# A unit's difference ahead of the low half of the unit in front, with other banks, pages and load times at the changes of stages and blocks

## The chip, the cores and the metric

The kernel runs on one core of a Trainium2 chip. The metric is the device time of one execution in microseconds (us), as the median of several runs. The core's engines work in parallel, each through its own queue in order: TensorE (PE; PEld is its loading of weights), VectorE (DVE), ScalarE (ACT), GpSimd (POOL) and SyncE (SP). SP and ACT also issue the DMA transfers.

## The reference

A linear attention with a normalisation of each row feeds two feed-forward layers, one behind the other, on 4608 tokens of width 512 with 2048 hidden channels:

```python
kv = einsum('bhsd,bhse->bhde', k, v); out = einsum('bhsd,bhde->bhse', q, kv)
x = out / sqrt(mean(out * out) + 1e-06) * g_norm      # then tokens x (heads * dim)
h = x @ w_in;  x = (h * sigmoid(h)) @ w_out           # moe
h = x @ w_in2; r = maximum(h, 0)
y = (s * (r * r) + b) @ w_out2                        # moe2
```

All is float32.

## The kernel before

**Numbers.** TensorE multiplies in a rounded format (`F32R`). To keep float32 accuracy each operand is split into a high half, the rounded value, made by ACT (`nc.scalar.copy`), and a low half, the value minus its high half, made by DVE (`nc.vector.tensor_sub`). A product is then three passes (`PASSES`, line 556): high by high, high by low, low by high.

**Stages.** There are four: stage 1 is the attention and `x @ w_in` with its activation (`emit_h`, in nine steps `j` of 512 tokens, 16 column groups `m` each); stage 2 is `@ w_out` (class `Output`); stage 3 is the second `@ w_in` with its activation (class `Hidden`); stage 4 the second `@ w_out` (`Output` again). Stages 2 to 4 work on five blocks of tokens, in the order 1, 2, 3, 4, 0: four long ones of two times 512 and a short one of two times 256. Each 2 by 2 block product there is done as seven products instead of eight (Strassen's scheme in Winograd's form), named in the order of their use P1, P5, P6, P2, P7, P4, P3. They add up in three kinds of PSUM banks, x, v and y: P1 and P2 in x, P5 and P3 in v, P6, P7 and P4 in y, to which x is copied first.

**The loop of stages 2 and 4** (`Output.run`, line 845). Its unit is a product k and one of NA = 4 groups a of channels, 28 units a block, 12 matmuls a unit (two halves q of the output, two channel groups i, three passes). `load` issues a unit's loads on SP, seven units ahead: r for P5, P2 and P7 into four pages in turn (`R_ROOMS`), sa for P6, ka for P1. `make` (line 763) makes the operand of a unit three units ahead into one of four slots (`RING`, one for each a): for P5, P6 and P7 first a difference on DVE (lines 774, 776, 778), then the high half on ACT (line 780) and the low half on DVE (line 781). For P2 the kept operand `ka` is changed behind the low half (line 783). At the end of a product `end_of` (line 819) copies or adds the banks: line 833 copies y at the end of P7, line 834 adds v, line 794 scales in stage 4, line 840 adds v and u at the end of P3. In stage 4 `rows_out` transposes finished rows (line 810), copies them on ACT (line 812) and stores them.

**Stage 3** (`Hidden.run`, line 690) goes through 40 groups g = (block, i), seven slots each, 6 matmuls a slot. P4 and P3 of a group come one group later. The operands of a block (7 splits into halves) are made by `split` (line 591), their sums T1, T2, T4 and B12 by `combine` (line 578). For the first block `before` (line 607) does that during the last, short block of stage 2; for the others `behind` does it in the last group of the block in front. Results go into a page (`G_ROOMS`, line 562, four in turn) by `square` on ACT or `add_square` on ACT and DVE (lines 685 to 688), and `defer` puts the store's issue on ACT's queue some slots later (`run_late`, once a slot). Between the slots the weights of stage 4 are prepared in small steps (`steps4`, called in `beside3`, line 936), and weight tiles are loaded (`grid[..].load`, line 312).

**Order.** All is in a manual schedule: each engine does its instructions in the order in which the code emits them; the framework adds the waits. A page or bank with a tag has one owner at a time, so a new owner waits until the last reader of the old one is done.

Of the kernel before, what the change touches and what calls it, by code (L numbers as in the profile page):

```python
# [8 lines left out]
F32 = mybir.dt.float32  # L9
# [8 lines left out]
def kernel(  # L18
# [37 lines left out]
    P = 128  # L56
# [402 lines left out]
    def emit_h(j, m):  # L459
# [8 lines left out]
        g = room(("gh_0", "gh_1", "gl_0", "gl_1")[m % 4], [P, T], F32, f"g{j}_{m}")  # L468
# [89 lines left out]
    class Hidden:  # L558
# [3 lines left out]
        G_ROOMS = ("sg_0", "sg_1", "sg_2", "v_1")  # L562
# [15 lines left out]
        def combine(self, b, o):  # L578
# [5 lines left out]
            elif o == self.T2:  # L584
                to, x, y = self.raw[b, self.T1], B22, self.raw[b, self.T1]
            else:
                to, x, y = self.raw[b, self.T2], self.raw[b, self.B21], self.raw[b, self.T2]
# [19 lines left out]
        def before(self, k, a):  # L607

            b = order[0]
            if (k, a) == (P7, 3):  # L610
                for o in (self.B11, self.B12, self.B22, self.B21):
                    self.load(b, o)
            if (k, a) == (P4, 1):
                self.combine(b, self.T1)
            if (k, a) == (P3, 0):
                self.split(b, P1)
            if (k, a) == (P3, 1):
                self.split(b, P5)
                self.combine(b, self.T2)
                self.split(b, P6)  # L620
            if (k, a) == (P3, 2):
                self.split(b, P2)
                self.combine(b, self.B12)
            if (k, a) == (P3, 3):
                self.split(b, P7)
# [44 lines left out]
        def out(self, g, f, h):  # L670
            b = self.seq[g][0]
            self.turn += 1
            r = room(self.G_ROOMS[self.turn % 4], [P, T], F32, f"g{b}_{f}_{h}")[:, :size[b]]
            defer(2 if b else 4, lambda: nc.scalar.dma_start(self.gt[b][f, h], r))
            return r

        def square(self, g, f, h, ps):
            r = self.out(g, f, h)
# [3 lines left out]
        def add_square(self, g, f, h, x, y):  # L682
            r = self.out(g, f, h)
# [37 lines left out]
    class Output:  # L721


        def __init__(self, stage):
            self.stage, self.grid, self.gt = stage, grid[stage], gt[stage - 1]
            self.units = [(b, k, a) for b in order for k in range(7) for a in range(NA)]
            self.loaded = self.made = 0
            self.s, self.r, self.o, self.acc, self.c, self.waiting = {}, {}, {}, {}, {}, []
            self.turn = 0
            self.keep, self.t = {}, []  # L730
            self.c_rooms = ["gh_0", "kvw1_0", "sg_2" if stage == 2 else "T", "v_0", "v_1", "sg_0", "sg_1", "gl_1"]
# [31 lines left out]
        def make(self, upto):  # L763
            while self.made < min(upto, len(self.units)):
                u = self.made
                self.made += 1
                b, k, a = self.units[u]
                n = size[b]
                o = self.o[u] = room(RING[a], [P, 2, 2, T], F32R, f"o{self.stage}_{u}")[:, :, :, :n]
                keep = self.kept(a, n)  # L770
                r = self.r.pop(u, None)
# [7 lines left out]
                x = r if k in (P2, P7) else s if k == P3 else keep  # L779
# [301 lines left out]
```

## Time and profile before

| | us |
|---|---|
| median of 3 runs | 1670.33 (1666.95 to 1672.37) |
| profiled execution | 1665.62 |
| its span | 1663.5 |
| PE matmul busy | 1593.3 |
| DVE busy | 957.2 |
| ACT busy | 802.5 |

The profile is of one execution. In a timeline a row is a run of like instructions: start, time, engine, line, operation, output and inputs, count, and in brackets the idle time of the engine just before it and what ended it. Matmuls overlap by some 0.15 us, so a row's time is longer than the distance to the next row's start. In a grouped row stand the busy time, the mean of one instruction, and the idle time before them with what ended it. The granted clock is a share of 2.4 GHz.

### The profile page before, as it was taken

How to read it: one execution, taken by the hardware profiler on the slowest of the kernel's cores; microseconds unless marked ns; L12 is line 12 of the kernel's file. 1: busy time of each engine (PE TensorE's matmuls, PEld its weight loads, DVE VectorE, ACT ScalarE, POOL GpSimd, SP SyncE). 2: the span in 40 equal slices, each digit the busy share in tenths (PEclk: the TensorE clock that was granted, in tenths of full speed). 3: DMA queues.
4: the chain of work that ended last, by engine and by line, in shares of the span. 5: the costliest groups of instructions: out<-in, count | busy, mean ns of one | idle time of the engine just before them, and what ended most of it. 6: DMA issues, size and time to landing. Idle time of an engine off the chain costs nothing.

```text
span 1663.5 us, 22083 instructions
## 1 busy us (share of the span) xinstructions
PE 1593.3 (96%) x8232; PEld 1309.2 (79%) x8232; DVE 957.2 (58%) x1298; ACT 802.5 (48%) x1310; POOL 1.6 (0%) x8
## 2 busy tenths in 40 slices
PE   7999999999899999999998999999989999999998
PEld 5778877888788778778787778787888787878787
DVE  5625544554321767676756666667545757575745
ACT  3645544555333343444444565656554454545454
POOL 0000000000000000000000000000000000000000
PEclk9999999999999999999999999999999999999999
DMA  8977887788829552626259747565467662626241
GB/s 240 279 221 255 277 269 253 244 287 264 329 83 335 182 215 89 228 78 240 80 197 360 279 179 260 189 238 195 184 236 288 251 237 67 225 66 236 65 152 51
DMA packets 228074, 349.60 MB, mean 210 GB/s; under 512 B 59008, under 2 KB 96896, under 8 KB 227968
## 3 DMA queue, kind: packets, MB, share of 16 engines
q1 hardware_dynamic: 145504, 209.49, 38.6%
q10 hardware_dynamic: 82464, 138.71, 22.3%
q8 instruction: 65, 1.06, 0.3%
q14 instruction: 41, 0.34, 0.1%
HBM read 209.72 MB, written 138.41 MB: 209 GB/s over the span
## 4 chain that ended last, share of the span: by engine, by line
PE 51%; DVE 21%; ACT 11%; DMA 10%; issue 5%; ACTq 1%; SPq 1%; DVEq 0%
PE ph L465 18%; DVE o L781 9%; PE qy L858 8%; ACT o L780 8%; PE py L662 7%; PE qv L858 5%; PE pv L662 4%; DMA gt<-g 4%; PE px L662 4%; DVE r L778 3%; DVE ka L774 3%; DVE ka L776 2%; DVE ka L783 1%; PE pkv L346 1%; PE po L371 1%
## 5 line engine op out<-in xcount | busy, mean ns | idle before, releaser
L858 PE MATMUL qy<-o,w 128*128 128x512 f32 (+1 forms) x1440 | 314.4, 373 | 23.8 <-DVE o L781 18.2
L858 PEld LDWEIGHTS qy<-o,w 128*128 128x128 f32 x1440 | 248.9, 188 | 86.3 <-DVE o L781 35.5
L781 DVE TENSOR_TENSOR o<-ka,o 128x1024 fp32r<-128x1024 f32 (+1 forms) x160 | 177.0, 1117 | 199.0 <-ACT o L780 188.3
L780 ACT CAST o<-ka 128x1024 fp32r<-128x1024 f32 (+1 forms) x160 | 152.0, 963 | 203.3 <-DVE ka L776 91.7
L858 PE MATMUL qv<-o,w 128*128 128x512 f32 (+1 forms) x960 | 203.5, 369 | 1.5 <-ACT o L780 0.9
L858 PE MATMUL qx<-o,w 128*128 128x512 f32 (+1 forms) x960 | 203.8, 370 | 0.0
L858 PEld LDWEIGHTS qv<-o,w 128*128 128x128 f32 x960 | 167.1, 189 | 31.5 <-ACT o L780 1.1
L858 PEld LDWEIGHTS qx<-o,w 128*128 128x128 f32 x960 | 168.0, 190 | 29.9
L662 PE MATMUL py<-x,w 128*128 128x512 f32 (+1 forms) x720 | 164.9, 374 | 12.2 <-ACT g L685 9.2
L465 PE MATMUL ph<-xh,wh 128*128 128x512 f32 x576 | 166.1, 410 | 6.9 <-ACT xh L443 5.3
L469 ACT ACTIVATE g<-ph 128x512 f32<-128x512 f32 x144 | 86.1, 598 | 150.6 <-PE ph L465 145.9
L662 PEld LDWEIGHTS py<-x,w 128*128 128x128 f32 x720 | 127.0, 191 | 39.6 <-ACT g L685 11.5
L465 PE MATMUL ph<-xl,wh 128*128 128x512 f32 x576 | 155.7, 392 | 0.0
L465 PE MATMUL ph<-xh,wl 128*128 128x512 f32 x576 | 154.5, 390 | 0.0
L780 ACT CAST o<-r 128x1024 fp32r<-128x1024 f32 (+1 forms) x80 | 75.0, 962 | 110.9 <-DVE r L778 110.9
L465 PEld LDWEIGHTS ph<-xl,wh 128*128 128x128 f32 x576 | 108.6, 189 | 24.6 <-DVE xl L444 0.4
L465 PEld LDWEIGHTS ph<-xh,wl 128*128 128x128 f32 x576 | 108.3, 188 | 23.4
L465 PEld LDWEIGHTS ph<-xh,wh 128*128 128x128 f32 x576 | 101.0, 189 | 27.2 <-ACT xh L443 6.8
L662 PE MATMUL pv<-x,w 128*128 128x512 f32 (+1 forms) x480 | 113.8, 373 | 5.1 <-issue 4.4
L781 DVE TENSOR_TENSOR o<-r,o 128x1024 fp32r<-128x1024 f32 (+1 forms) x80 | 89.3, 1116 | 44.0 <-ACT o L780 44.0
L662 PE MATMUL px<-x,w 128*128 128x512 f32 (+1 forms) x480 | 111.9, 369 | 0.0
L662 PEld LDWEIGHTS pv<-x,w 128*128 128x128 f32 x480 | 85.8, 192 | 21.3 <-issue 4.8
(114 smaller groups left out, 1635.5 us busy)
## 6 DMA issues: line engine op xcount, KB each, us to landing
gt<-g ACTq DMA_DIRECT2D x272, 256.0 KB, 2.6
r<-gt SPq DMA_DIRECT2D x96, 512.0 KB, 4.4
w<-wd SPq DMA_DIRECT2D x84, 512.0 KB, 6.6
wd<-wo ACTq DMA_DIRECT2D x112, 256.0 KB, 4.2
wr<-in_moe_w_in_dram SPq DMA_DIRECT2D x16, 1024.0 KB, 6.1
wr<-in_moe_w_out_dram SPq DMA_DIRECT2D x16, 1024.0 KB, 5.4
ka<-gt SPq DMA_DIRECT2D x32, 512.0 KB, 5.3
sa<-gt SPq DMA_DIRECT2D x32, 512.0 KB, 8.5
```

The costliest lines, as they stand in the source:

```text
L346: nc.tensor.matmul(ps[r, r], kc, vc, start=(c == 0), stop=(c == SC))
L371: nc.tensor.matmul(po[off:off + n, p * P:(p + 1) * P], qT_t[t][:, p, off:off + n], kvw[b % 2][:, p, :], start=True, stop=True,)
L465: nc.tensor.matmul(ps, wt[:, c, :], xt[:, c, :], start=(n == 0 and c == 0), stop=(n == 2 and c == KT - 1))
L469: nc.scalar.activation(g, ps, AF.Silu)
L662: nc.tensor.matmul(ps, a[:, s, c], x[t][c], start=(k in (P1, P5) and n == c == 0), stop=(n == 2 and c == 1), skip_group_check=True,)
L774: nc.vector.tensor_sub(keep, r, keep)
L776: nc.vector.tensor_sub(keep, s, keep)
L778: nc.vector.tensor_sub(r, s, r)
L780: nc.scalar.copy(o[:, :, 0], x)
L781: nc.vector.tensor_sub(o[:, :, 1], x, o[:, :, 0])
L783: nc.vector.tensor_sub(keep, r, keep)
L858: nc.tensor.matmul(ps, t[:, s], self.o[u][:, i, p], start=(k in (P1, P5) and a == i == m == 0), stop=(a == NA - 1 and i == 1 and m == 2), ...
```

## The change

- `Output.make` is cut in two. `prepare` makes a unit's difference, for P2 also the changed `ka`; `make` makes the halves. In `run` the next unit's `prepare` is called between a unit's high and low half, so on DVE a unit's difference stands ahead of the low half of the unit in front.
- In stage 2 the v banks are y2 and y3 instead of y0 and y1.
- The operands of stage 3's first block are loaded two units sooner; T2 gets a page of its own for that block, and T1, T2, the P6 split and B12 move to the P4 units; one split is left for each P3 unit.
- Stage 3's results in the short block go through seven pages instead of four, their stores are issued 3 or 4 slots later instead of 4; in the long blocks the stores of `add_square` 3 slots later instead of 2. One weight step less is done in each long block, at the last but one group's P4.
- Stage 1's results go through eight pages instead of four, and in the last step but one through twelve of their own.

```diff
         def run(self, behind):
             for u, (b, k, a) in enumerate(self.units):
                 self.load(u + 7)
-                self.make(u + 4)
+                self.make(u + 4, 1)
...
-        def make(self, upto):
+        def prepare(self, upto):
+            while self.prepared < min(upto, len(self.units)):
+                u = self.prepared
+                self.prepared += 1
+                self.load(u + 1)
...
                 elif k == P7:
                     nc.vector.tensor_sub(r, s, r)
-                x = r if k in (P2, P7) else s if k == P3 else keep
+                elif k == P2:
+                    nc.vector.tensor_sub(keep, r, keep)
+                self.x[u] = r if k in (P2, P7) else s if k == P3 else keep
+
+        def make(self, upto, ahead=0):
+            while self.made < min(upto, len(self.units)):
+                u = self.made
+                self.made += 1
+                self.prepare(u + 1)
...
                 nc.scalar.copy(o[:, :, 0], x)
+                self.prepare(u + 1 + ahead)
                 nc.vector.tensor_sub(o[:, :, 1], x, o[:, :, 0])
-                if k == P2:
-                    nc.vector.tensor_sub(keep, r, keep)
...
-                        self.acc[kind, q] = bank(f"a_{q}" if kind == "x" else f"y{q}_0", f"q{kind}{self.stage}_{b}_{q}")
+                        self.acc[kind, q] = bank(f"a_{q}" if kind == "x" else f"y{self.v0 + q}_0", f"q{kind}{self.stage}_{b}_{q}")
...
+            self.v0 = 2 if stage == 2 else 0
...
-            if (k, a) == (P7, 3):
+            if (k, a) == (P7, 1):
                 for o in (self.B11, self.B12, self.B22, self.B21):
                     self.load(b, o)
-            if (k, a) == (P4, 1):
-                self.combine(b, self.T1)
-            if (k, a) == (P3, 0):
-                self.split(b, P1)
-            if (k, a) == (P3, 1):
-                self.split(b, P5)
-                self.combine(b, self.T2)
+            if k == P4 and a < 2:
+                self.combine(b, (self.T1, self.T2)[a])
+            if (k, a) == (P4, 2):
                 self.split(b, P6)
-            if (k, a) == (P3, 2):
-                self.split(b, P2)
                 self.combine(b, self.B12)
-            if (k, a) == (P3, 3):
-                self.split(b, P7)
+            if k == P3:
+                self.split(b, (P1, P5, P2, P7)[a])
...
-                to, x, y = self.raw[b, self.T1], B22, self.raw[b, self.T1]
+                to = pair("wf_0", f"xt2_{b}")[:, :, :size[b]] if b == order[0] else self.raw[b, self.T1]
+                x, y = B22, self.raw[b, self.T1]
...
-        G_ROOMS = ("sg_0", "sg_1", "sg_2", "v_1")
+        G_ROOMS = ("sg_0", "sg_1", "sg_2", "v_1", "v_0", "kvw1_0", "gh_0")
...
-            r = room(self.G_ROOMS[self.turn % 4], [P, T], F32, f"g{b}_{f}_{h}")[:, :size[b]]
-            defer(2 if b else 4, lambda: nc.scalar.dma_start(self.gt[b][f, h], r))
+            r = room(self.G_ROOMS[self.turn % (4 if b else 7)], [P, T], F32, f"g{b}_{f}_{h}")[:, :size[b]]
+            defer(slots if b else slots + 1, lambda: nc.scalar.dma_start(self.gt[b][f, h], r))
             return r
 
         def square(self, g, f, h, ps):
-            r = self.out(g, f, h)
+            r = self.out(g, f, h, 2)
...
         def add_square(self, g, f, h, x, y):
-            r = self.out(g, f, h)
+            r = self.out(g, f, h, 3)
...
-            if 0 < i < NF - 1 and k not in (P1, P3):
+            if 0 < i < NF - 1 and k not in (P1, P3) and (i, k) != (NF - 2, P4):
                 do_some(steps4, 1)
...
-        g = room(("gh_0", "gh_1", "gl_0", "gl_1")[m % 4], [P, T], F32, f"g{j}_{m}")
+        pages = ("gh_0", "gh_1", "gl_0", "gl_1")
+        if j < NB - 2:
+            pages += ("W4", "W5", "W6", "W7")
+        tag = f"W{m}" if j == NB - 2 and m < 3 * NA else pages[m % len(pages)]
+        g = room(tag, [P, T], F32, f"g{j}_{m}")
```

## Rows read from the trace of the kernel before

**Rows 1.** The page: busy us, share of the span and instructions of each engine.

```profile
PE 1593.3 (96%) x8232; PEld 1309.2 (79%) x8232; DVE 957.2 (58%) x1298; ACT 802.5 (48%) x1310; POOL 1.6 (0%) x8
```

**Rows 2.** Timeline of PE in stage 2, as described above.

```profile
536.72 11.04 PE L858 MATMUL qx<-o,w 128*128 128x512 f32 x48
547.60 11.04 PE L858 MATMUL qv<-o,w 128*128 128x512 f32 x48
...
569.27 2.79 PE L858 MATMUL qy<-o,w 128*128 128x512 f32 x11 [0.54 <-DVE o L781]
...
647.92 2.79 PE L858 MATMUL qy<-o,w 128*128 128x512 f32 x11 [0.55 <-DVE o L781]
...
872.32 5.92 PE L858 MATMUL qx<-o,w 128*128 128x256 f32 x48
878.08 3.47 PE L858 MATMUL qy<-o,w 128*128 128x256 f32 x25
```

**Rows 3.** Timeline of PE from stage 2 to stage 3.

```profile
897.07 1.55 PE L662 MATMUL px<-x,w 128*128 128x512 f32 x6
903.00 2.90 PE L662 MATMUL pv<-x,w 128*128 128x512 f32 x6 [4.38 <-issue]
```

**Rows 4.** Grouped lines of PE in stage 2 (536 to 897.2 us).

```profile
L858 PE MATMUL qy<-o,w 128*128 128x512 f32 (+1 forms) x720 | 156.2, 372 | 8.6 <-DVE o L781 8.5
```

**Rows 5.** Timeline of DVE in stage 2: units of P6, then of P2.

```profile
557.33 1.23 DVE L781 TENSOR_TENSOR o<-ka,o 128x1024 fp32r<-128x1024 f32 x1 [1.19 <-ACT o L780]
558.47 1.22 DVE L776 TENSOR_TENSOR ka<-sa,ka 128x1024 f32<-128x1024 f32 x1
560.88 1.23 DVE L781 TENSOR_TENSOR o<-ka,o 128x1024 fp32r<-128x1024 f32 x1 [1.19 <-ACT o L780]
...
570.27 1.22 DVE L783 TENSOR_TENSOR ka<-r,ka 128x1024 f32<-128x1024 f32 x1
571.40 1.22 DVE L781 TENSOR_TENSOR o<-r,o 128x1024 fp32r<-128x1024 f32 x1
```

**Rows 6.** Grouped lines of PE in stage 4 (from 1268 us).

```profile
L858 PE MATMUL qy<-o,w 128*128 128x512 f32 (+1 forms) x720 | 158.2, 373 | 15.1 <-DVE o L781 9.7 <-ACT c L833 5.4
```

**Rows 7.** Timeline of ACT at the end of P7 in a block of stage 4.

```profile
1413.17 0.81 ACT L794 ACTIVATE c<-c,sums,scol 128x512 f32<-128x512 f32 x1 [1.94 <-DVE c L834]
```

**Rows 8.** The page's DMA issues: count, KB each, median us to landing.

```profile
r<-gt SPq DMA_DIRECT2D x96, 512.0 KB, 4.4
```

**Rows 9.** Windows: busy us of PE, PEld, DVE, ACT, POOL, then clock, DMA share, GB/s.

```profile
903.00:908.30 5.30, 5.30 (x13) 4.14 (x14) 2.60 (x3) 1.29 (x2) 0.00 (x0) 0.50 1.04 410
```

**Rows 10.** Timeline of DVE at the end of stage 2.

```profile
890.53 1.23 DVE L589 TENSOR_TENSOR xt<-xs,xs 128x1024 f32<-128x1024 f32 x1 [1.87 <-DMA xs<-yt]
...
902.48 0.75 DVE L840 TENSOR_TENSOR c<-qv,qu 128x256 f32<-128x256 f32 x2
```

**Rows 11.** Timeline of SP's DMA issues at the end of stage 2.

```profile
881.87 4.61 SPq L576 DMA_DIRECT2D xs<-yt  x4
```

**Rows 12.** Timeline of PE at a change of blocks in stage 3.

```profile
1139.70 3.09 PE L662 MATMUL py<-x,w 128*128 128x512 f32 x12 [1.07 <-ACT g L685]
```

**Rows 13.** Timeline of ACT just before that.

```profile
1138.11 1.05 ACT L604 CAST x<-xs 128x1024 fp32r<-128x1024 f32 x1 [2.11 <-DVE g L688]
```

**Rows 14.** Grouped lines of PE in stage 3's short block (1213 to 1262 us).

```profile
L662 PE MATMUL py<-x,w 128*128 128x256 f32 (+1 forms) x149 | 22.5, 295 | 5.2 <-ACT g L685 2.6 <-ACT u L706 2.6
```

**Rows 15.** Waits of ACT there (1215 to 1270 us): total, times, longest.

```profile
ACT g L679 <- DMA gt<-g: 11.5, 6, 4.0
```

**Rows 16.** Timeline of PE at the end of stage 3.

```profile
1265.60 1.65 PE L662 MATMUL py<-x,w 128*128 128x256 f32 x6 [3.39 <-ACT g L685]
```

**Rows 17.** Timeline of ACT just before that.

```profile
1263.47 1.04 ACT L780 CAST o<-ka 128x1024 fp32r<-128x1024 f32 x1 [1.40 <-DMA ka<-gt]
1265.18 0.37 ACT L685 COPY g<-py 128x256 f32<-128x256 f32 x1 [0.66 <-DMA gt<-g]
```

**Rows 18.** Grouped lines of PE over the whole span: stage 1's first pass.

```profile
L465 PE MATMUL ph<-xh,wh 128*128 128x512 f32 x576 | 166.1, 410 | 6.9 <-ACT xh L443 5.3 <-ACT g L469 1.6
```

More of the change, by code (lines that the diff above doesn't have):

```diff
@@ L668, in of, with out @@
             return self.banks[kind, g][:, :size[self.seq[g][0]]]
-        def out(self, g, f, h):
+        def out(self, g, f, h, slots):
             b = self.seq[g][0]
             self.turn += 1
-            r = room(self.G_ROOMS[self.turn % 4], [P, T], F32, f"g{b}_{f}_{h}")[:, :size[b]]
-            defer(2 if b else 4, lambda: nc.scalar.dma_start(self.gt[b][f, h], r))
+            r = room(self.G_ROOMS[self.turn % (4 if b else 7)], [P, T], F32, f"g{b}_{f}_{h}")[:, :size[b]]
+            defer(slots if b else slots + 1, lambda: nc.scalar.dma_start(self.gt[b][f, h], r))
             return r
         def square(self, g, f, h, ps):
-            r = self.out(g, f, h)
+            r = self.out(g, f, h, 2)
             nc.scalar.activation(r, ps, AF.Relu)
@@ L726, in __init__ @@
             self.units = [(b, k, a) for b in order for k in range(7) for a in range(NA)]
-            self.loaded = self.made = 0
-            self.s, self.r, self.o, self.acc, self.c, self.waiting = {}, {}, {}, {}, {}, []
+            self.loaded = self.prepared = self.made = 0
+            self.s, self.r, self.x, self.o, self.acc, self.c, self.waiting = {}, {}, {}, {}, {}, {}, []
             self.turn = 0
             self.keep, self.t = {}, []
+            self.v0 = 2 if stage == 2 else 0
             self.c_rooms = ["gh_0", "kvw1_0", "sg_2" if stage == 2 else "T", "v_0", "v_1", "sg_0", "sg_1", "gl_1"]
@@ L761, in load @@
                     )
-        def make(self, upto):
-            while self.made < min(upto, len(self.units)):
-                u = self.made
-                self.made += 1
+        def prepare(self, upto):
[3 more added lines that the diff above has]
+                self.load(u + 1)
                 b, k, a = self.units[u]
                 n = size[b]
-                o = self.o[u] = room(RING[a], [P, 2, 2, T], F32R, f"o{self.stage}_{u}")[:, :, :, :n]
-                keep = self.kept(a, n)
-                r = self.r.pop(u, None)
+                keep, r = self.kept(a, n), self.r.get(u)
                 s = self.s[a][:, :, :n] if a in self.s else None
@@ L778, in make @@
                     nc.vector.tensor_sub(r, s, r)
-                x = r if k in (P2, P7) else s if k == P3 else keep
+                elif k == P2:
[6 more added lines that the diff above has]
+                self.prepare(u + 1)
+                b, k, a = self.units[u]
+                o = self.o[u] = room(RING[a], [P, 2, 2, T], F32R, f"o{self.stage}_{u}")[:, :, :, :size[b]]
+                x = self.x.pop(u)
                 nc.scalar.copy(o[:, :, 0], x)
+                self.prepare(u + 1 + ahead)
                 nc.vector.tensor_sub(o[:, :, 1], x, o[:, :, 0])
-                if k == P2:
-                    nc.vector.tensor_sub(keep, r, keep)
                 if k == P4 and u + 2 * NA < len(self.units):
```

## The prediction

> **What bounds the kernel now.** I read the busy shares first. TensorE (PE) is busy for 96% of the span [rows 1], so at most some 70 us can be won, and only where PE waits; VectorE (DVE) at 58% and ScalarE (ACT) at 48% matter only where PE waits for them. So I went through the PE timeline stage by stage. A stall-free run of 48 products of 512 columns takes 10.88 us from start to start, 0.2267 us each, and one of 256 columns 5.76 us, 0.120 each [rows 2]. A block of 512 columns is 28 units of 12 products, 76.16 us (2.72 a unit); the short block is 40.32 us (1.44 a unit).
>
> Stage 2 runs from 536.72 to 897.07 us, 360.35 us [rows 2, 3], for 4 x 76.16 + 40.32 = 344.96 us of products: 15.39 us are lost. A steady block shows the pattern: between the stalls at 569.27 and 647.92 us, one block apart, lie 78.65 us, so 2.49 us are lost a block [rows 2]. The grouped lines name the cause: the qy products stood idle for 8.6 us, 8.5 of them behind the low half on line 781 [rows 4]. An idle time is only what exceeds the overlap of two products, so 8.6 us of idle time stand for 15.39 us lost, a factor of 1.79.
>
> Why the low half is late is seen on DVE [rows 5]. For a unit of P5, P6 or P7, DVE makes the difference, waits 1.19 us for ACT to round it (the high half), and only then subtracts for the low half: 3.55 us from low half to low half (557.33 to 560.88), against 2.72 us that PE needs. Eight such units in a row, P5 and P6, eat up the lead of three units. Where nothing is waited for (P2, 570.27 to 571.40), DVE does one operation in 1.13 us beside ACT's rounding.
>
> Then I read the change from stage 2 to 3, the blocks of stage 3, and stage 4, which has the same loop as stage 2.
>
> **1. The difference ahead of the low half in front.** Nothing is added or removed: the same 16 differences and 28 low halves a block, in another order on DVE. DVE then does the next difference while ACT rounds, so a unit costs it 2 x 1.14 = 2.28 us (about 1.2 in the short block) against 2.72 (1.44) for PE. PE is late next, which is the bound wanted. For P2 the kept difference moves ahead of the low half; that unit had no wait. Stage 2: of 15.39 us I take 14 (bounds 9 and 15.4), as the short block keeps little reserve, 1.2 against 1.44.
>
> Stage 4: PE's qy products are idle 9.7 us behind line 781 and 5.4 us behind line 833 [rows 6]. By the factor 1.79 the first are 17.4 us. The second are five waits, one a block: the copy of y for q = 1 stands on ACT behind the scaling for q = 0, which waits for a DVE add, which stands behind DVE's late low halves (the scaling at 1413.17 us, after 1.94 us of waiting) [rows 7]. When these are on time the copy is ready within the 1.36 us in which PE does the q = 0 half, so I count 5.4 + 5 x 0.28 = 6.8 us, 0.28 being what a stall loses beyond its idle time in stage 2's steady blocks. Some 2 us more are lost in the short last block behind row copies that wait for their stores; those stay, as their order does not change. Of 24.2 us I take 23 (bounds 15 and 26).
>
> What is newly queued: a difference that waits for its load now holds back the low half of the unit in front. The load of P7 unit a goes into the page of P2 unit a, which is free when that unit's low half is done, about 2.2 us into the block's tenth unit (one unit later for each a). The low half held back, that of the unit before P7's, is due 11.8 us later in a long block, 6.2 us in the short one. The median load lands 4.4 us after its issue [rows 8], so I cost this at nothing; bounds 0 and, in crowded stretches, some 3 us a block.
>
> The Trainium skill speaks against this edit at one point: TensorE: Matmul & The Clock Gate, in the table at its head, gives VectorE a strictly ordered queue, so that a waiting instruction stops all behind it. That is the mechanism of the first rival below. By the rows here the load has 11.8 us for 4.4, and the sum stands.
>
> **2. Other banks and times between stage 2 and 3.** PE stops for 4.38 us before the first pv product and then runs at a granted clock of 0.50 (1.2 instead of 2.4 GHz) for 5.3 us [rows 3, 9]. The six products from 897.07 us are worth 6 x 0.2267 = 1.36 us and the next starts at 903.00, so 4.57 us are lost, and half of 5.3 us by the clock: 4.57 + 2.65 = 7.2 us. DVE's line 840 at 902.48 us is what frees bank y0_0 [rows 10]; it stood in DVE's queue behind slots' low halves and combinations. With v in y2 and y3, stage 3's first pv needs no such release. Next late is the P5 slot itself, whose low half comes about 1 us before it is needed, then P7's. P6, T2 and B12 move from the P3 units into P4, so DVE's eight long operations at 1.14 us are four in each; with eight short low halves at 0.6 they need 13.9 us of PE's 11.5 in P4 and P3, and the lead covers most of the rest. I take 6.4 of 7.2 (bounds 0 and 7.2; the moved waits below are the lower bound).
>
> The four loads of xs leave the SP queue two units sooner, so exactly one weight load (that of the 20th unit) comes behind them instead of ahead. They wait for pages that P7's low halves free, and these come earlier too. In the trace SP issues them from 881.87 us and the first combination starts at 890.53 us, after 1.87 us of waiting on DVE [rows 10, 11].
>
> On this, the Trainium skill says (Trainium Kernel Development and Optimization, Key Constraints) that transfers of all queues share the same 16 DMA engines and interleave. The DMA share there is 1.04 [rows 9], so a shift past one weight load is worth about one load; no more is counted.
>
> **3. Stage 3.** At a change of blocks PE waits about 1 us for line 685 (1.07 at 1139.70 us) [rows 12], because ACT stood 2.11 us behind DVE's line 688 in order to issue a store [rows 13]. That store moves one slot back, and one weight step leaves that place: three such changes, 3 us in all, of which I take 2.5 (bounds 0 and 4). The longer hold of a page costs a slot, 1.36 us; the store lands before the page is due again, four slots later, so I add nothing. In the short block PE's py products are idle 5.2 us behind lines 685 and 706 [rows 14], and ACT waits 11.5 us for stores to land before a page is free [rows 15]. Seven pages instead of four nearly double the time to land: with four stalls 5.8 us lost, I take 5 (bounds 3 and 6). The last stall, 3.39 us [rows 16], mostly stays: ACT waits for ka before it and only the 0.7 us behind a page goes [rows 17].
>
> **4. Pages in stage 1.** In the whole stage PE idles 1.6 us behind line 469 [rows 18], so four more pages are worth 0 to 1.6 us; I take 0.
>
> **Sum.** 14 + 23 + 6.4 + 2.5 + 5 + 0.7 = 51.6 us. The profiled execution took 1665.62 us (span 1663.5 and 2.1 around it), which would become 1614.0. The median of the runs is 1670.33, 4.7 above it; with the same offset I predict 1618.7 us.
>
> **Rivals.** *The difference waits for its load.* In the crowded stretches (first and last block of stages 2 and 4, DMA near 1.0) loads take far longer than 4.4 us, and the low halves behind them return as stalls of 2 to 3 us a block: 11 us back, 1630 us. For it: xs took over 8 us [rows 10, 11]. Against it: 11.8 us are allowed in a long block.
>
> *The combinations hold up P3.* T1 moves one unit ahead; in the trace it waits 1.87 us for xs with low halves of P3 queued behind it [rows 10]. If xs lands as late as now, 12.4 us after P7's start (878.08 to 890.53 us) [rows 2, 10], the low half of the first P3 unit, then behind T1, is out at about 12.4 + 1.14 + 0.6 = 14.2 us and due at 8 x 1.44 = 11.5: PE stops 2.7 us, the P3 units behind it are short too, and if the clock falls again as in [rows 9], the 6.4 us are not won: 1625 us.
>
> *It does not do what it says.* The ring of four slots, not DVE's order, could hold the high half. Then line 781 still stalls PE and only parts 2 and 3 remain, some 15 us and what little part 1 gives: 1652 us. Against it: P2's units run without a wait.
>
> *Slower than before: the loads bind.* If a load from the page's release to its landing takes over 11.8 us in every block, each group of four differences makes PE wait for what is over. To eat 51.6 us and 5 more in the ten blocks of stages 2 and 4 it must be 5.7 us over, 17.5 us against the median of 4.4: 1675 us or more. From some 17 us on it decides.
>
> **How the numbers follow.** Forecast 0.70, difference waits 0.09, combinations 0.10, does nothing 0.04, loads bind 0.07 (0.04 beyond 1675 us, 0.03 about even). A change within 0.3%, 5 us, can't be told from none here. Faster 0.93, same 0.03, slower 0.04. The forecast's own bounds give some 1608 to 1628 us; up to the first rival's 1630 and a little beyond it is 1608 to 1634.
>
> **What would show it.** Right: blocks of 76.2 to 76.5 us in stage 2, no idle time behind line 781, DVE's low halves without a gap in P5 to P7, no gap and no clock of 0.50 near the start of stage 3, the 833 waits of stage 4 under 0.3 us. Wrong: DVE waiting at lines 774, 776 or 778 (under their new numbers) for r or sa, a gap in P3 of the last block of stage 2, ACT waiting for landing stores in stage 3's short block.

## The result and the profile after

The changed kernel takes 1609.14 us (median of four runs, 1606.38 to 1613.92) against 1671.35 us for the kernel before (four runs, one more than in the table above); the ratio is 0.9635, with a 95% interval of 0.9605 to 0.9665. Its profiled execution took 1609.3 us, with a span of 1607.5, against 1665.62 and 1663.5. Line numbers shift by the change: 781 is now 794, 780 is 792, 833 is 844, 794 is 805, 840 is 851, 662 is 661, 679 is 678, 685 is 684, 706 is 705, 469 is 473.

Both spans can be cut at the first product of each stage and of each block. Everything below goes by this table, in us, of one profiled execution of each kernel; the blocks stand in the order in which they run, the short one last.

| | before | after | difference | predicted |
|---|---|---|---|---|
| stage 1 (to the first qx) | 536.7 | 531.0 | -5.7 | 0 |
| stage 2 | 360.4 | 347.9 | -12.4 | -14 |
| its blocks | 80.21, 78.65, 78.65, 78.65, 44.19 | 4 x 76.16, 43.27 | | |
| stage 3 | 371.3 | 354.1 | -17.2 | -14.6 |
| its blocks | 86.85, 77.75, 78.02, 75.53, 53.11 | 78.78, 76.33, 76.16, 74.87, 47.96 | | |
| stage 4 | 395.1 | 374.5 | -20.7 | -23 |
| its blocks | 83.94, 84.57, 85.13, 84.48, 57.03 | 81.10, 80.27, 80.28, 80.28, 52.53 | | |
| span | 1663.5 | 1607.5 | -56.0 | -51.6 |

The page of the changed kernel, busy us, share of the span and instructions of each engine [rows 1]:

```profile
PE 1574.7 (98%) x8232; PEld 1311.9 (82%) x8232; DVE 958.5 (60%) x1298; ACT 811.9 (51%) x1310; POOL 1.6 (0%) x8
```

DVE has the same instructions and nearly the same busy time. Only their order changed, and PE waits less. The timeline of PE in stage 2 (start, us, engine, line, operation, shapes, count) answers [rows 2]: from block to block it is 683.36 - 607.20 = 76.16 us, the ideal.

```profile
607.20 11.04 PE L869 MATMUL qx<-o,w 128*128 128x512 f32 x48
...
683.36 11.04 PE L869 MATMUL qx<-o,w 128*128 128x512 f32 x48
```

The grouped lines of PE in stage 2 (busy us, mean ns, idle us before them and its releasers), as in [rows 4]: the 8.6 us ahead of qy are gone; 2.2 us stand ahead of qv.

```profile
L869 PE MATMUL qy<-o,w 128*128 128x512 f32 (+1 forms) x720 | 149.5, 368 | 0.0
L869 PE MATMUL qv<-o,w 128*128 128x512 f32 (+1 forms) x480 | 101.0, 368 | 2.2 <-DVE o L794 2.2
```

DVE's timeline in stage 2, units of P6, against [rows 5]: difference and low half follow one another, and what it still waits for is 0.35 us of ACT's rounding. From low half to low half it is 2.72 us (551.41 to 554.13), PE's own pace; it was 3.55.

```profile
549.84 1.22 DVE L776 TENSOR_TENSOR ka<-sa,ka 128x1024 f32<-128x1024 f32 x1
551.41 1.23 DVE L794 TENSOR_TENSOR o<-ka,o 128x1024 fp32r<-128x1024 f32 x1 [0.35 <-ACT o L792]
552.56 1.22 DVE L780 TENSOR_TENSOR ka<-r,ka 128x1024 f32<-128x1024 f32 x1
554.13 1.23 DVE L794 TENSOR_TENSOR o<-ka,o 128x1024 fp32r<-128x1024 f32 x1 [0.36 <-ACT o L792]
```

From stage 2 to 3, PE's timeline against [rows 3]: no stop before the first pv product, and the granted clock from 878.95 to 884 us is 1.00. But ahead of the change, in P3, the low half is late by 1.84 us at 876.10.

```profile
870.83 3.43 PE L869 MATMUL qv<-o,w 128*128 128x256 f32 x24 [0.32 <-DVE o L794]
876.10 3.02 PE L869 MATMUL qv<-o,w 128*128 128x256 f32 x23 [1.84 <-DVE o L794]
878.95 1.55 PE L661 MATMUL px<-x,w 128*128 128x512 f32 x6
880.34 1.52 PE L661 MATMUL pv<-x,w 128*128 128x512 f32 x6
```

DVE's timeline shows why: T1 waited 2.66 us for xs, and P6's low half and the combination B12 stand ahead of the low half (875.36) that PE wants.

```profile
868.95 1.23 DVE L594 TENSOR_TENSOR xt<-xs,xs 128x1024 f32<-128x1024 f32 x1 [2.66 <-DMA xs<-yt]
...
873.08 1.23 DVE L610 TENSOR_TENSOR x<-xt,x 128x1024 fp32r<-128x1024 f32 x1 [0.57 <-ACT x L609]
874.22 1.22 DVE L594 TENSOR_TENSOR xs<-xs,xs 128x1024 f32<-128x1024 f32 x1
875.36 1.28 DVE L794 TENSOR_TENSOR o<-sa,o 128x512 fp32r<-128x512 f32 x2
```

The grouped lines of PE in stage 4 (from 1233 us) answer [rows 6]: of 15.1 us idle ahead of qy, 1.5 are left, 0.25 in each long block and 0.5 in the last.

```profile
L869 PE MATMUL qy<-o,w 128*128 128x512 f32 (+1 forms) x720 | 150.9, 369 | 1.5 <-ACT c L844 1.5
```

In stage 3's short block (1185 to 1233 us) PE's py products are idle 4.3 us, the stop at its end included, where they were idle 5.2 + 3.4 us [rows 14, 16], and ACT waits 0.8 us for a store to land ahead of line 678 [rows 15]. At its end PE still stops behind the copy that stands on ACT behind the rounding of ka [rows 16, 17]. Below: a grouped line of PE, a wait of ACT (total, times, longest), a row of PE's timeline.

```profile
L661 PE MATMUL py<-x,w 128*128 128x256 f32 (+1 forms) x150 | 22.4, 295 | 4.3 <-ACT g L684 2.3 <-ACT u L705 2.1
...
ACT g L678 <- DMA gt<-g: 0.8, 1, 0.8
...
1230.29 1.65 PE L661 MATMUL py<-x,w 128*128 128x256 f32 x6 [2.26 <-ACT g L684]
```

### The profile page after: what moved, and what is told of

Read it like the earlier page. It is cut to its first block, busy times and chain, and to the rows that moved or that the text cites. A ratio compares the mean times of both kernels' runs of the same rounds, so it can differ in the third digit from the quotient of the medians.

```text
span 1607.5 us, 22036 instructions
## 1 busy us (share of the span) xinstructions
PE 1574.7 (98%) x8232; PEld 1311.9 (82%) x8232; DVE 958.5 (60%) x1298; ACT 811.9 (51%) x1310; POOL 1.6 (0%) x8
## 4 chain that ended last, share of the span: by engine, by line
PE 70%; DMA 4%; DVE 2%; ACT 1%; issue 1%; ACTq 0%; SPq 0%; DVEq 0%
PE qy L869 16%; PE qx L869 12%; PE qv L869 11%; PE py L661 9%; PE ph L465 9%; PE pv L661 6%; PE px L661 6%; DMA r<-gt 1%; PE pt L821 1%; DMA wd<-wp 1%; DVE o L794 1%; DMA kv<-in_k_dram 1%; PE po L371 1%; DMA xs<-yt 0%; DMA w<-wd 0%
## 5 line engine op out<-in xcount | busy, mean ns | idle before, releaser
L869 PE MATMUL qy<-o,w 128*128 128x512 f32 (+1 forms) x1440 | 300.4, 368 | 1.5 <-ACT c L844 1.5
L794 DVE TENSOR_TENSOR o<-r,o 128x1024 fp32r<-128x1024 f32 (+1 forms) x80 | 89.4, 1118 | 35.8 <-ACT o L792 35.7
```

What stands on the lines that cost most here:

```text
L794: nc.vector.tensor_sub(o[:, :, 1], x, o[:, :, 0])
L869: nc.tensor.matmul(ps, t[:, s], self.o[u][:, i, p], start=(k in (P1, P5) and a == i == m == 0), stop=(a == NA - 1 and i == 1 and m == 2), ...
```

## Experiments

**Part 1 alone, and everything but part 1.** The first kernel is the one before with `prepare` and `make(u + 4, 1)` added and v in the banks y0 and y1. The second is the changed kernel with one line turned back:

```diff
-                self.make(u + 4, 1)
+                self.make(u + 4)
```

> The kernel before with part 1 alone (the difference of the next unit ahead of the low half). My theory, that the order on DVE is the whole cause of the idle time behind the low halves: the loss of stage 2 falls from 15 to about 1 us, that of the four long blocks of stage 4 from 18.9 to about 4, the short last block from 8.5 to 4, so 33 to 35 us in all and about 1637 us, with the stop of PE between stages 2 and 3 (4.4 us and the half clock), the block changes of stage 3 and its short block as before. Rival, that part 1 needs the other banks and pages to pay off (a difference kept waiting by loads that stand behind others): stalls stay in the first and last blocks, a gain of 25 us or less, 1646 or more. Second rival, that freeing pages earlier repairs the change of stages by itself: the stop at the start of stage 3 goes too, 1630 or less.

> The changed kernel with the differences back in the place right before their own rounding; all else of the change stays. My theory: the stalls behind the low half return, 2.5 us a block in stage 2 and 4.6 to 5.2 in stage 4, in all 33 to 35 us: about 1643 us. If the two parts lean on each other, more than 38 us (the stop between stages 2 and 3 comes back as well, 1650); if other parts of the change carry the gain, under 28 us (1637).

Part 1 alone: 1630.47 us, ratio 0.9775 (0.9741 to 0.9809), 37 us less than the kernel before in the same round (1667.86), where I expected a gain of 33 to 35. Without it: 1644.27 us, ratio 0.9847 (0.9817 to 0.9877), as expected. In the traces part 1 alone takes stage 2 from 360.4 to 346.2 us and stage 4 from 395.1 to 372.8, so 14.1 and 22.3 us where 14 and 23 had been predicted; the changed kernel without it has stages of 362.1 and 393.3 us. The grouped qy lines of PE in stage 2, with part 1 alone and then without it, say the same:

```profile
L870 PE MATMUL qy<-o,w 128*128 128x512 f32 (+1 forms) x720 | 149.5, 368 | 0.0
```

```profile
L869 PE MATMUL qy<-o,w 128*128 128x512 f32 (+1 forms) x720 | 156.3, 372 | 8.7 <-DVE o L794 8.5
```

So the order on DVE was the cause, and it needs none of the other edits. The second rival (that earlier pages repair the change of stages too) falls: with part 1 alone the stop is there, unchanged at 4.38 us.

```profile
889.23 2.90 PE L662 MATMUL pv<-x,w 128*128 128x512 f32 x6 [4.38 <-issue]
```

**How many pages the ahead needs.** The changed kernel with three, then two pages for the loads r, which are issued a unit or two later to suit:

```diff
-    R_ROOMS = ("XA", "XB", "Q", "K")
+    R_ROOMS = ("XA", "XB")
...
-                    r = self.r[u] = pair(R_ROOMS[self.turn % 4], f"r{self.stage}_{u}")[:, :, :n]
+                    r = self.r[u] = pair(R_ROOMS[self.turn % 2], f"r{self.stage}_{u}")[:, :, :n]
...
-                self.load(u + 7)
+                self.load(u + 5)
```

> The changed kernel with three pages instead of four for the loads r of stages 2 and 4 (the loads are issued a unit later, as far as the pages allow). A difference made ahead then waits for a load into the page that the low half two places ahead of it frees, so DVE needs 4.4 (landing, by the profile) + 1.14 + 1.14 = 6.7 us for two units, 3.34 a unit against PE's 2.72, over seven units: 4.3 us, which the lead of three units (8 us) covers. My theory: the long blocks stay at 76.2 to 76.5 us in stage 2 and the short blocks lose 1 to 3 us: 1609 to 1615. Rival of the prediction, that the loads bind: 2 us or more lost in every long block, 1628 or more.

> The same with two pages. The difference made ahead waits for a page that the low half right in front of it in DVE's queue has just freed: landing, difference and low half follow one another, 4.4 + 1.14 + 1.14 = 6.7 us a unit against 2.72. Over the seven units of P2 and P7 behind the first that is 28 us, less the lead of 8: some 20 us a long block and 10 to 15 a short one, in all about 180 us: some 1790, slower than the kernel before. That is the rival on the slower side with its condition made true. If SP has the loads out early enough anyhow, less than 5 us a block and under 1660.

Two pages: 1783.31 us in one run, and the blocks of stage 2 take 93.3, 94.2, 92.7, 94.5 and 59.6 us, 16 to 18 us a block over the changed kernel. DVE's timeline there shows the serial chain: landing, difference, low half, 6.1 to 6.3 us a unit.

```profile
581.32 1.23 DVE L778 TENSOR_TENSOR r<-sa,r 128x1024 f32<-128x1024 f32 x1 [5.26 <-DMA r<-gt]
582.46 1.22 DVE L794 TENSOR_TENSOR o<-r,o 128x1024 fp32r<-128x1024 f32 x1
587.60 1.23 DVE L778 TENSOR_TENSOR r<-sa,r 128x1024 f32<-128x1024 f32 x1 [3.92 <-DMA r<-gt]
588.75 1.22 DVE L794 TENSOR_TENSOR o<-r,o 128x1024 fp32r<-128x1024 f32 x1
```

The difference for the next unit stands at the head of DVE's queue, waiting for a load into the page that was only just released, and the finished high half's low half waits behind it: ACT's rounding from 582.65 us took 1.04 us, and its low half ran at 588.75. The Trainium skill (TensorE: Matmul & The Clock Gate, the table at its head) says of VectorE's queue that it is strictly ordered. The trace agrees: the low half stood behind the 3.92 us of waiting in front of 587.60. That it is the page and not the later call of `load` is seen on SP, whose issues of r wait for the low half that frees the page (575 to 620 us; total, times, longest):

```profile
SPq L755 <- DVE o L794: 24.1, 4, 7.2
```

With three pages the long blocks of stage 2 stay at 76.16 us, as forecast, and the short blocks lose more than the 1 to 3 us that I gave them: 58.29 against 52.53 us in stage 4, and 47.78 in stage 2, where the changed kernel takes 43.27 and others with the same instructions there up to 46.3; 1622.00 us, ratio 0.9718 (0.9690 to 0.9745). PE's timeline in the short block of stage 2, three pages:

```profile
859.76 1.70 PE L869 MATMUL qx<-o,w 128*128 128x256 f32 x12 [0.70 <-DVE o L794]
...
863.76 1.69 PE L869 MATMUL qy<-o,w 128*128 128x256 f32 x12 [0.43 <-DVE o L794]
```

So "the loads bind" is a true mechanism, and two pages meet its condition and make the kernel slower than before. With four pages the long blocks have a page to spare; in the short ones DVE waits a little for loads.

**Banks or order between stages 2 and 3.** The changed kernel with v in y0 and y1 again; and the changed kernel with `before` and T2's page as they were, but v in y2 and y3.

```diff
-            self.v0 = 2 if stage == 2 else 0
+            self.v0 = 0
```

> The changed kernel with the v products of stage 2 back in the banks y0 and y1; the earlier loads, combinations and roundings between stages 2 and 3 stay. The prediction credits the banks with the 4.4 us stop and the half clock. In the changed kernel DVE's addition that frees these banks ends at about 880.7 us and PE wants the bank at 880.3. Theory, that the order of the work on DVE is enough by itself: a stop of 0.5 to 1 us, no fall of the clock, the first block of stage 3 within 1.5 us of 78.8 us, about 1610. Rival, that the banks did it: the stop of 4 us and the clock of 0.50 return, the first block of stage 3 takes 84 to 86 us, 1615 or more.

> The changed kernel with the loads, combinations and roundings between stages 2 and 3 at their old units; the other banks stay. Theory, that either the banks or the order alone removes the stop: the first pv product of stage 3 follows without the stop of 4 us; the late roundings of P6 and P7 cost 1 to 3 us in the first slots, and the last block of stage 2 is 1.7 us shorter (41.6 instead of 43.3 us): 1608 to 1611. Rival, that the order did it alone: the stop returns and the first block of stage 3 takes 84 us or more, 1614 or more.

Old banks: 1612.96 us, ratio 0.9667 (0.9648 to 0.9686); old order: 1614.76, ratio 0.9676 (0.9654 to 0.9697). The times hardly separate them, the traces do. With the old banks PE goes on without a stop (first block of stage 3: 80.25 us):

```profile
883.77 1.52 PE L661 MATMUL px<-x,w 128*128 128x512 f32 x6
885.13 1.52 PE L661 MATMUL pv<-x,w 128*128 128x512 f32 x6
```

With the old order the bank is free, pv starts on time, and PE stops one slot later, for 3.55 us; then the granted clock is 0.50 (first block: 84.87 us). Below: PE's timeline, the window (us of PE, PEld, DVE, ACT, POOL, clock, DMA share, GB/s) and ACT's timeline.

```profile
883.36 1.52 PE L666 MATMUL pv<-x,w 128*128 128x512 f32 x6
888.43 2.93 PE L666 MATMUL py<-x,w 128*128 128x512 f32 x6 [3.55 <-ACT py L705]
...
888.40:892.00 3.60, 3.57 (x8) 2.81 (x9) 1.74 (x2) 0.60 (x2) 0.00 (x0) 0.50 1.03 399
...
886.70 1.04 ACT L608 CAST x<-xs 128x1024 fp32r<-128x1024 f32 x1 [2.69 <-DVE xs L593]
887.81 0.57 ACT L705 COPY py<-px 128x512 f32<-128x512 f32 x1
```

The copy that PE wants is behind a rounding that waits for B12 on DVE. So the order removes the stop and the banks alone only put another release in its place. How much it brings is less sure. The last block of stage 2 and the first of stage 3 together take 131.0 us before, 127.0 with part 1 alone and 122.1 in the changed kernel, but 122.8 to 126.7 in four other kernels that are the same there (those of the experiment on stage 1, below): what is left of part 2 beside part 1 is 0.2 to 4.9 us, not 6.4. With the old banks the two take 126.3 us, within that spread, so no gain of the other banks is shown; with the old order they take 129.1, outside it.

Part of the spread is the clock behind the stop in P3. The last block of stage 2 takes 43.3, 43.7 and 45.1 us in three kernels that are the same there and show a granted clock of 1.00 over that block, and 44.9, 45.5 and 46.3 us in three more that show 0.96. With W0 to W11 alone (below) the same stop as in the changed kernel, 1.83 us long, is followed by a clock of 0.50. PE's timeline and a window there:

```profile
874.08 4.51 PE L867 MATMUL qv<-o,w 128*128 128x256 f32 x23 [1.83 <-DVE o L792]
...
875.00:877.00 2.00, 2.00 (x12) 2.00 (x11) 1.89 (x2) 0.45 (x1) 0.00 (x0) 0.50 1.02 400
```

**Stage 3 as before.** The changed kernel with four pages, the old slots and the weight step at its old place:

```diff
-        G_ROOMS = ("sg_0", "sg_1", "sg_2", "v_1", "v_0", "kvw1_0", "gh_0")
+        G_ROOMS = ("sg_0", "sg_1", "sg_2", "v_1")
...
-            defer(slots if b else slots + 1, lambda: nc.scalar.dma_start(self.gt[b][f, h], r))
+            defer(2 if b else 4, lambda: nc.scalar.dma_start(self.gt[b][f, h], r))
```

> The changed kernel with stage 3 as before: four pages for its results in all blocks, stores issued at the old slots, and the weight step at its old place. My theory: the 1 us stalls at the three changes of blocks return (about 3 us in all with the one near 940 us), and the short block loses 11 instead of 6 us: 8 to 9 us, about 1617.5. Rival: with part 1 in place stage 4 and the low halves leave ACT and DVE freer and the stalls of stage 3 don't return in full: 3 us or less, 1612.

1624.74 us, ratio 0.9737 (0.9709 to 0.9766). Blocks 2 to 4 of stage 3 take 77.77, 77.72 and 75.52 us against 76.33, 76.16 and 74.87: 3.7 us. The short block with the first of stage 4 takes 136.8 us against 129.1: 7.7. Both are more than forecast. But with part 1 alone, where stage 3 is the old one too, these two blocks take 133.6 us, 4.6 more than in the changed kernel; the changes of blocks cost 3.7 there as well. PE's grouped py line from 1192 to 1249 us, a wait of ACT, and PE's last stop:

```profile
L661 PE MATMUL py<-x,w 128*128 128x256 f32 (+1 forms) x150 | 24.7, 316 | 9.6 <-ACT g L684 9.1 <-ACT u L705 0.3
...
ACT g L684 <- DMA gt<-g: 8.1, 3, 3.7
...
1246.34 1.65 PE L661 MATMUL py<-x,w 128*128 128x256 f32 x6 [4.59 <-ACT g L684]
```

After such stops the granted clock is below 1 (0.93 from 1185 to 1210 us, 0.88 from 1210 to 1250, where the changed kernel has 1.00 and then 0.89 to 1235), which I had not priced in the short block. It is also what parts the two kernels with the old stage 3: PE stops for 9.6 and 9.3 us in the short block, but the granted clock over it is 0.89 here and 0.97 with part 1 alone. So what part 3 is worth there lies between 4.6 and 7.7 us, by how far the clock falls.

**Pages of stage 1.** Four kernels. The first is the changed one with the old pages, as in the first diff; the second keeps W4 to W7 and gives up W0 to W11; the third does the reverse; the fourth has the old pages and, as in the second diff, takes the loads of stage 2's weights out of the last block but one.

```diff
-        if j < NB - 2:
-            pages += ("W4", "W5", "W6", "W7")
-        tag = f"W{m}" if j == NB - 2 and m < 3 * NA else pages[m % len(pages)]
+        tag = pages[m % len(pages)]
```

```diff
-        if j == NB - 2 and m >= 4:
-            grid[2].load()
...
-            if m >= 2:
-                grid[2].load()
+            grid[2].load(2 if m < 6 else 1)
```

> The changed kernel with the four pages of the kernel before for the results of stage 1. Stage 1 became 5.7 us shorter, where I had counted 0 to 1.6 us for pages. My theory: most of the 5.7 us came from how transfers happened to land in the block from 420 to 446 us of that one execution and not from the pages; without them the time is within 2 us of 1609 and stage 1 has 1.6 us or less behind the line that makes g, 1611 at most. Rival: the pages did it; stage 1 ends 4 to 7 us later than in the changed kernel and the time is 1613 to 1616.

> The changed kernel without one half of the edit in stage 1: in the last block but one of stage 1 the results lie in the four old pages again instead of W0 to W11; the pages W4 to W7 in the blocks ahead of it stay. In the changed kernel the loads of stage 2's weights, which go to W0 to W11, start at 444 us instead of 410, because their pages hold results; the DMA share from 415 to 435 us is 0.4 to 0.6 instead of 1.03. Theory, that this later start is what the edit is worth: the stalls near 425 to 442 us return, 5 to 9 us, stage 1 takes 536 us or more, about 1616. Rival, that more pages in the blocks ahead did it: stage 1 stays within 2 us of 531, 1611 at most.

> The changed kernel without the other half of the edit in stage 1: the results of the last block but one lie in W0 to W11, the blocks ahead of it have the four old pages again. With W4 to W7 alone the 5th to 12th load of stage 2's weights started at 436.8 us and later, instead of 414.8 to 430, and the stalls near 425 to 442 us were gone; so each half holds back loads. Theory of the later start: here no load starts before some 440 us, and the seventh and eighth block of stage 1 take about 55.7 and 51.0 us as in the changed kernel. Rival, that the pages in the blocks ahead matter: the two take 60 and 52 us or more, as in the kernels with the old pages.

> The changed kernel with all the old pages of stage 1, but with the loads of stage 2's weights moved: none in the last block but one of stage 1, and two at each of the first six steps of the last block, then one a step. If the theory of the later start holds, this does the same as the pages: no stall at 425 to 442 us, stage 1 near 531 us, 1607 to 1612 us in all. Rival, that the pages are needed (the results wait for their stores): the stalls stay, stage 1 takes 536 us or more, 1616.

| kernel | time, us | stage 1's 7th and 8th block | DMA share, 415 to 435 us |
|---|---|---|---|
| before | 1671.35 | 61.1 + 51.2 | 1.03 |
| part 1 alone | 1630.47 | 60.3 + 52.8 | 1.03 |
| old pages | 1618.88 | 64.9 + 53.8 | 1.02 |
| W4 to W7 alone | 1614.27 | 55.9 + 51.0 | 0.77 |
| W0 to W11 alone (one run) | 1609.66 | 55.9 + 51.0 | 0.54 |
| old pages, loads moved | 1616.95 | 57.1 + 54.2 | 0.55 |
| changed kernel | 1609.14 | 55.7 + 51.0 | 0.48 |

My expectation for the old pages was wrong: the 5.7 us are no accident. Every kernel with the old pages and the old loads has the stalls, and none with the new pages has them. PE's timeline with the old pages:

```profile
428.05 0.63 PE L439 MATMUL px<-ident,xnp 128*128 128x128 f32 x4 [2.24 <-DVE xnp L413]
...
436.34 0.66 PE L439 MATMUL px<-ident,xnp 128*128 128x128 f32 x4 [1.73 <-DVE xl L444]
...
447.77 2.08 PE L465 MATMUL ph<-xh,wh 128*128 128x512 f32 x4 [4.82 <-ACT xh L443]
```

None of these waits names line 469 (now 473), by which I had priced the edit. What differs is on SP's queue: when the weights of stage 2 are fetched. Its rows (start, time from first to last issue, count) in the kernel before, in the changed one, with W4 to W7 alone, and with W0 to W11 alone:

```profile
409.67 20.90 SPq L312 DMA_DIRECT2D w<-wd  x12
```

```profile
444.29 37.26 SPq L312 DMA_DIRECT2D w<-wd  x12
```

```profile
413.74 38.09 SPq L312 DMA_DIRECT2D w<-wd  x12
```

```profile
440.71 37.37 SPq L312 DMA_DIRECT2D w<-wd  x12
```

In the kernel before, twelve loads of 512 KB go out in 21 us, just when ACT issues its stores; the DMA share is 1.03, and on ACT the rounding xh that PE needs stands for 4.16 us behind a store's issue, at 430.93 us, that waits until an earlier store, issued at 422.98, has landed at 430.85 (timeline of ACT, kernel before):

```profile
431.30 0.69 ACT L443 ACTIVATE xh<-px,gcol 128x512 fp32r<-128x512 f32 x1 [4.16 <-DMA wd<-wo]
```

In the changed kernel the pages W0 to W11 hold results, and each load waits until the store of the result in its page has landed: the first goes out at 444.29 us, and that store landed at 444.23. The windows of the two kernels, 415 to 435 us, before and after:

```profile
415.00:435.00 20.00, 17.85 (x85) 14.28 (x84) 9.89 (x25) 6.61 (x12) 0.00 (x0) 1.00 1.03 395
```

```profile
415.00:435.00 20.00, 20.00 (x98) 16.53 (x97) 13.87 (x33) 9.88 (x19) 0.00 (x0) 1.00 0.48 182
```

The run with the old pages and moved loads is the test: no further page, and no stall left at 425 to 442 us. So it is the time of the loads and not the pages. It missed its forecast of 1612 all the same: two loads a step moved the crowd into the next block (share 1.04 from 437 to 455 us), and the two blocks together take 111.3 us, not 106.7:

```profile
448.85 1.19 PE L465 MATMUL ph<-xh,wh 128*128 128x512 f32 x4 [1.94 <-ACT g L469]
```

With W4 to W7 alone I had expected the stalls back. They did not come, since the loads from the fifth on also went out late, from 436.77 us, and the trace tells why: they are the loads into W4 to W7, which hold the last four results of the seventh block, and each waits for its page's store. These stores landed at 436.71, 442.54, 445.09 and 449.48 us, and the loads went out at 436.77, 442.60, 445.15 and 449.55; the last four followed by 451.39. SP's waits there (425 to 455 us; total, times, longest):

```profile
SPq L312 <- DMA gt<-g: 32.5, 4, 21.0
```

With W0 to W11 alone no load goes out before 440.71 us, and the two blocks are those of the changed kernel, as expected. The Trainium skill (Trainium Kernel Development and Optimization, Key Constraints) says that transfers of all queues share 16 DMA engines; here the share of 1.03 with SP's loads and ACT's stores in it, and 0.48 without the loads, agree.

**Two further edits.** The changed kernel with the work at both changes of stages moved back a little:

```diff
-            if k == P4 and a < 2:
-                self.combine(b, (self.T1, self.T2)[a])
-            if (k, a) == (P4, 2):
-                self.split(b, P6)
-                self.combine(b, self.B12)
+            if k == P4 and a > 0:
+                self.combine(b, (self.T1, self.T2, self.B12)[a - 1])
             if k == P3:
-                self.split(b, (P1, P5, P2, P7)[a])
+                self.split(b, (P1, P5, P6, P2)[a])
+            if (k, a) == (P3, 3):
+                self.split(b, P7)
...
-            if k in (P1, P5, P2, P7):
-                out4.make({P1: 1, P5: 2, P2: 3, P7: 4}[k])
+            if k in (P1, P5, P4, P3):
+                out4.make({P1: 1, P5: 2, P4: 3, P3: 4}[k])
```

> The changed kernel with two further edits. First: between stages 2 and 3 the combinations T1, T2, B12 one unit later each, and the rounding of P6 behind that of P5 in P3. In the changed kernel DVE does P6's rounding (873.08 us, after 0.57 of waiting) and B12 (874.22) ahead of the low half that PE waits for 2.00 us at 876.10, and T1 waits 2.66 us for its load ahead of the one PE waits for 0.48 us. Second: at the end of stage 3 the rounding of units 3 and 4 of stage 4 comes behind P4 and P3 instead of P2 and P7; ACT waits for the load of ka ahead of the copy that PE waits for 2.26 us at 1230.29 us, and PE then runs at a clock of 0.50 for some 6 us. My theory: the stops go and no new ones take their place: 2.5 us in stage 2, 2.4 and about 3 us by the clock at the start of stage 4, so 6 to 8 us less, about 1602. Rival, that the queues are full there and the stops only move: P6, P7 or the first units of stage 4 stop PE instead, 1607 to 1611.

1606.76 us (1605.69 to 1610.99), ratio 0.9631 (0.9610 to 0.9652): it missed the 1602 that I expected, and the time does not separate it from the changed kernel. By the trace the second edit holds: the stop at the end of stage 3 is 0.46 us, and the short block and the next one take 124.1 us, where the nine others with the new stage 3 and the old place of these roundings have 127.1 to 129.5 (not counting the kernel with two pages). The first edit is as its rival said: the stalls in P3 are gone (that block takes 40.60 us), but PE stops for 0.88 us in stage 3, and the two blocks together take 122.05 us, what the changed kernel took. As the four kernels that are the same there as the changed one took 122.8 to 126.7, whether this edit gains something stays open.

```profile
881.26 1.52 PE L660 MATMUL pv<-x,w 128*128 128x512 f32 x6
883.65 1.66 PE L660 MATMUL py<-x,w 128*128 128x512 f32 x6 [0.88 <-ACT py L699]
...
1231.74 0.98 PE L660 MATMUL py<-x,w 128*128 128x256 f32 x6 [0.46 <-ACT g L683]
```

## Why the prediction was right, and where it was off

The direction was right, and the range held the time, by about 1 us at its lower end. Of what was to show it, the block times and the start of stage 3 came as written. The rest came nearly so: in the long blocks no idle time is left behind line 781, but 2.2 us in P3 of the last block of stage 2 and 0.3 in the last block of stage 4; DVE's low halves have gaps of 0.35 us instead of 1.19 in P6; the 833 waits are 0.25 us in the long blocks of stage 4 and 0.5 in the short one. Of the signs against it, the gap in P3 came, ACT's wait for a landing store came once, with 0.8 us, and DVE's waits for loads came almost only in the short blocks. For the profiled execution I had 1614.0 us and it took 1609.3. For the median I had 1618.7 and it is 1609.1: half of that difference is the offset of 4.7 us between the profiled execution and the median of the kernel before. I carried it over, and it is not a property of the kernel: the changed one's profiled execution lies 0.2 us from its median. The other half comes from stage 1, which I had priced at nothing and which gave 5.7 us. Stages 2 to 4 gave 50.3 us for the 51.6 that I had added up; that they agree so well is in part luck, as the misses below have both signs.

- **Part 1, 37 us: right.** Alone it gave 14.1 + 22.3 = 36.4 us. The long blocks of stage 2 are at 76.16 us, and DVE's low halves go at PE's pace. In the changed kernel stages 2 and 4 show 12.4 and 20.7: what part 2 moved into P4 lets P3 of the last block take 8.7 us where it took 7.0 with part 1 alone, and stage 4 begins at a clock of 0.50 (1230 to 1236 us), with a first block of 81.1 us against 79.7.
- **Part 2, 6.4 us: too much, and its cause misread.** I credited the banks. The stop goes with the order of the combinations and roundings; with the new banks and the old order it is back, behind the next release in line. The rival of the combinations came true in part: T1 waited 2.66 us for xs, and P3 took 8.7 us for 5.8 us of products. The fall of the clock that it named did not follow in the changed kernel's profiled execution, but it did in three of five others that are the same there.
- **Part 3, 8.2 us: right, or too little.** Without it 3.7 us return at the changes of blocks, of which I had 2.5, and 4.6 to 7.7 at the short block and behind it, of which I had 5.7. I took the idle times and left out that PE runs at a lower clock after such stops, by an amount that differs between executions.
- **Part 4, 0 us: wrong.** It measured 5.6 us: 112.3 us for the 7th and 8th block of stage 1 before, 106.7 after; against the other two kernels with the old pages and loads it is 6.4 and 12.0. I priced pages by the idle time behind the line that fills them. The edit's effect was on another queue: it postponed the loads that share those pages, and those loads had been holding up ACT's stores. For part 1 the prediction asked what is newly queued behind a wait; the same question here would have led there.
- **The slower side.** The loads do not bind in long blocks: in stage 2 three pages suffice there. In the short blocks DVE's waits for loads are small but there (1.8 us for sa and 1.7 for P7's r in the short block of stage 2), which is the first rival, at a small size.

## What to carry to other kernels

Where an engine makes two operations per unit and the second waits for another engine, let it do the next unit's first operation in between: it costs no instruction, and its price is that a late load now holds back a finished unit, so count the pages: landing + both operations, divided by the pages that are in flight (one less than there are), should stay under the consumer's pace. With two pages it was 6.1 to 6.3 us against 2.72; with three, 3.3 by estimate ((4.4 + 1.14 + 1.14) / 2), the lead of three units still covered it in the long blocks. Freeing one resource at a stop only helps if the next release in line is early: look at what would end the wait then. When a page changes hands, ask which transfer was waiting to use it, since the time of that transfer can be worth more than the page.

## What the runs showed of the hardware that I had not expected

The time from the start of the execution to the second block of stage 1 lies between 93.9 and 98.2 us in nine kernels whose instructions are the same up to there. Their first product of stage 1's first pass starts between 35.8 and 38.0 us, and over the block that follows the granted clock is 1.00 in four of them (58.0 to 60.4 us) and 0.96 or 0.97 in five (60.0 to 61.1 us). So a part of the difference goes with the clock. It is as large as the smaller parts of this change, so these had to be read stage by stage and not from times.

Nor does the length of a stop settle what the clock does behind it. The last block of stage 2 took 43.3 to 46.3 us in six kernels that are the same there. Each stops in P3; with the changed kernel the clock stays at 1.00 after a stop of 1.84 us, and with W0 to W11 alone it falls to 0.50 after one of 1.83. What parts the two, these runs don't show.
